# Weight pieces decoded two at a time through both banks of one PSUM tile, in an attention and MLP kernel on one Trainium2 core

## The chip, the cores and the metric

The kernel runs on one core of a Trainium2 chip. The core has TensorE (PE, matrix products), VectorE (DVE), ScalarE (ACT), GpSimd (POOL) and SyncE (SP, which only issues transfers here), each with a queue of its own that works in order; they meet through semaphores. SBUF is the memory on the core, PSUM the accumulators' memory, which is divided into banks of 512 fp32 columns. The metric is the device time of one execution in microseconds (us); lower is better.

## The reference

```python
# attention: B, H, S, D = 4, 8, 576, 64, top 32 scores of each row
scores = (q @ k.T) / sqrt(D)
kth = np.partition(scores, -32, axis=-1)[..., -32:-31]
scores = np.where(scores >= kth, scores, -1e9)
attn = softmax(scores)
x = (attn @ v)            # -> (2304, 512)
# first MLP, w_in (512, 2048), w_out (2048, 512)
h = x @ w_in
x = (h * sigmoid(h)) @ w_out
# second MLP, same sizes
h = x @ w_in
g = np.where(h > 0, h, np.exp(np.minimum(h, 0)) - 1)
out = g @ w_out
```

The inputs are float64, handed over as pairs of 32-bit integers, so that the kernel has to make floats of them itself.

## The kernel before

**Number format.** A float32 value is split into a high and a low fp16 part, and a product is three matmuls (high x high, high x low, low x high).

**Weights.** The four weight matrices come as 64 pieces (four matrices j, 16 pieces n each). A raw piece is 128 x 1024 int32, 512 KB: 512 numbers of two words per partition. Three VectorE operations decode it to 128 x 512 floats: L258 masks and shifts the high words into `y`, L262 ORs three bits of the low words into `y`, L265 takes the sign from the high words and writes the result `f`. `y` is a PSUM tile of the pool `ps_h` in slots 2 to 12, and `f` itself in the slots before and after. Then ScalarE squares the piece for a norm (L158), later scales it (L161), and GpSimd splits it into fp16 parts (L300, L164), in place in the large tile `W`, so that its row of raw words can take the next piece. Seven pieces of the last matrix are too late to find a place of their own; they come as two halves of 256 columns each (`halves`), most of which are staged in tiles of the MLP (t, gh, u, xt).

**The order of the work** is written out by hand: `slot(s)` records what the engines do in slot s, and the engines' queues keep this order. A slot has one attention tile out of 144 (18 chunks of 128 rows x 8 heads): the scores S by TensorE (L463), four rounds of MAX (L495) and MATCH_REPLACE (L499) on VectorE to find the 32nd largest, the exp on ScalarE (L510), the mask on VectorE (L523). `dv` interleaves the operations of tile s (list `a`) with those of tile s-1 (list `b`), and behind each of the eight sets `per` operations of the list `dec`, the slot's share of the decode. `d0` to `d3` say in which slot each piece is decoded: matrix 0 in slots -3 to 1, matrix 1 in slots 1 to 4, matrix 2 in 5 to 8, matrix 3 in 9 to 13.

**The MLP** begins in slot 13 (layer 0, LAG) and 25 (layer 1, LAG + LAG2). A slot has at most one step: 48 matmuls into a PSUM tile `h` of one bank (L633, 128 x 512), which ScalarE reads twice (L647 and L648 in layer 0, L652 and L653 in layer 1: first `u<-h`, then `t<-h`); GpSimd makes `t` of the two (L661), ScalarE and GpSimd make its fp16 parts `gh` (L665, L164), and 12 matmuls two slots later add it to the chunk's sum `a` (L681). Four steps make a chunk of a layer; then ScalarE copies `a` out to `o` (L694 or L725), before the next chunk may begin its sum. TensorE's order in a slot is `h`, `av` (the attention's product with V, L577), `a`, S of the next tile.

The pool `ps_h` has two buffers of one bank, so a step may write one while ScalarE still reads the other. In the decode the same two buffers hold the `y` of two neighbouring pieces, whose operations alternate (`in_turn`).

Of the kernel before, what the change touches and what calls it, by code (L numbers as in the profile page):

```python
# [10 lines left out]
F32 = mybir.dt.float32  # L11
F16 = mybir.dt.float16
BF16 = mybir.dt.bfloat16
I32 = mybir.dt.int32
# [3 lines left out]
PSUM = bass.MemoryType.PSUM  # L18
# [13 lines left out]
def kernel(  # L32
# [23 lines left out]
    NWP = KFF  # L56
# [5 lines left out]
    def pool(name, bufs, **kw):  # L62
        return ctx.enter_context(tc.tile_pool(name=name, bufs=bufs, **kw))
# [23 lines left out]
    dram = pool("dram", 1, space=bass.MemoryType.DRAM)  # L87
    p2_p = pool("p2", 6)
    ps_s = pool("ps_s", 2, space=PSUM)
    ps_h = pool("ps_h", 2, space=PSUM)  # L90
    ps_a = pool("ps_a", 1, space=PSUM)
    ps_v = pool("ps_v", 1, space=PSUM)

    W = const.tile([128, 4 * NWP + 1, 2 * DM], F16, name="W")
    Wraw = W.bitcast(F32)
    Wi = W.bitcast(I32)
    WEND = 4 * NWP + 1
# [22 lines left out]
    def xc(ch):  # L120
        kind, b, c = chunks[ch]
        return b if kind == "f" else B + b // 2
# [85 lines left out]

    stage3 = [1, 2, 3, 4, 1, 2, 3, 4, "tt", "gg", "ux", 1, "tt", "ug", (3 * NWP, WEND - 1), "gx"]

    def stage(where):
        if isinstance(where, int):
# [8 lines left out]
    weights = [w.bitcast(I32) for w in (w_in1, w_out1, w_in2, w_out2)]  # L223
    raws = {}

    def w_load(j, n, e=None):
        if j % 2 == 0:
            r0, c0 = (n % KDM) * 128, (n // KDM) * 1024
        else:
            r0, c0 = n * 128, 0  # L230
        if j < 2:
            r = 2 * NWP + 1 + 2 * n
        elif j == 2:
            r = 3 * NWP + 1 + 2 * (n % (NWP // 2))
        elif e is None:
            r = WEND - 2 * stage3[n]
        if e is None:
            t = Wi[:, r:r + 2, :].rearrange("p a x -> p (a x)")
            m = 1024
        else:  # L240
            t = stage(stage3[n][e])
            m = 512
            c0 = e * m
        nc.sync.dma_start(out=t, in_=weights[j][r0:r0 + 128, c0:c0 + m])
        raws[j, n, e] = t

    def w_dec_ops(j, n, e=None, psum=False):
        t = raws.pop((j, n, e)).rearrange("p (x two) -> p x two", two=2)
        f = Wi[:, j * NWP + n + 1, :]
        if e is not None:  # L250
            f = f[:, e * 256:(e + 1) * 256]
        low, high = t[:, :, 0], t[:, :, 1]
        y = [f]

        def first():
            if psum:
                y[0] = ps_h.tile([128, 512], F32, tag="h", name="h").bitcast(I32)[:, 0:f.shape[1]]
            nc.vector.tensor_scalar(y[0], high, 0x07FFFFFF, 3, op0=ALU.bitwise_and, op1=ALU.logical_shift_left)  # L258

        return [  # L260
            first,
            lambda: nc.vector.scalar_tensor_tensor(  # L262
                y[0], low, 29, y[0], op0=ALU.logical_shift_right, op1=ALU.bitwise_or
            ),
            lambda: nc.vector.scalar_tensor_tensor(  # L265
                f, high, -(1 << 30), y[0], op0=ALU.bitwise_and, op1=ALU.bitwise_or
            ),
        ]
# [350 lines left out]
    def emit_in(l, ch, i):  # L619
        if (l, i) == (0, 0):  # L620

            t = small.tile([128, 1], F32, tag="c1", name="c1")
            nc.gpsimd.tensor_scalar(t, ixs[:, xc(ch):xc(ch) + 1], sW[0][1], 0.5, op0=ALU.mult, op1=ALU.mult)
            c1[ch] = t
        xt = xts[l, ch]
        ps = ps_h.tile([128, 512], F32, tag="h", name="h")
        for u in range(4):
            for kk in range(KDM):
                n = 2 * l * NWP + i * 4 + kk
                f = u * 128  # L630
                wh, wl = W[:, n, f:f + 128], W[:, n, 512 + f:512 + f + 128]
                for x, (w, z) in enumerate(((wh, kk), (wh, KDM + kk), (wl, kk))):
                    nc.tensor.matmul(  # L633
                        out=ps[:, f:f + 128],
                        lhsT=w,
                        rhs=xt[:, z, :],
                        start=(kk == 0 and x == 0),
                        stop=(kk == KDM - 1 and x == 2),
                    )
        hps[l, ch, i] = ps  # L640
# [104 lines left out]
    LAG = 13  # L745
# [8 lines left out]
    loads, sumsq, tiny, early, splits, late, low, decs = (defaultdict(list) for _ in range(8))  # L754
# [18 lines left out]
    for (b, i), t in first_use.items():  # L773
        x = dict(b=b, i=i)
# [6 lines left out]
        else:  # L781
            d = 2 if b == 1 else 4
            r = first[b] - 17 - 8 * (d - 2) + 2 * d * i
# [7 lines left out]
    for g in range(NTILE // 2):  # L791
        t = 2 * g
# [3 lines left out]
    wload, wnow = defaultdict(list), defaultdict(list)  # L796

    def w_plan(j, dec, split):
        end = max(dec.values()) + 1
        for x, s in dec.items():  # L800
            decs[s].append((j, *x))
        for n in range(NWP):
            late[max(s for x, s in dec.items() if x[0] == n)].append((partial(w_norm, j, n), None))

        def total():
            m = w_sum(j)
            due.append((m, lambda m: early[end].append(lambda: w_ops(j, m))))

        late[end - 1].append((total, None))
        for (n, _), x in spread(end, split).items():  # L810
            late[x].append((partial(w_scaled, j, n), None))
            splits[x + 1].append(partial(w_split, j, n))
        return dec

    def spread(s, counts):
        return {(n, None): s + x for n, x in enumerate(x for x, c in enumerate(counts) for _ in range(c))}

    d0 = w_plan(0, spread(-3, (3, 3, 4, 4, 2)), (4, 4, 4, 4))
    d1 = w_plan(1, spread(1, (3, 5, 5, 3)), (4, 4, 4, 4))
    d2 = w_plan(2, spread(5, (4, 4, 4, 4)), (5, 5, 6))  # L820
    halves = {8: 11, 9: 11, 10: 11, 12: 12, 13: 12, 14: 13, 15: 13}
    d3 = spread(9, (4, 4, 4, 2, 2))
    d3 = w_plan(
        3, {(n, e): s for (n, _), s in d3.items() for e in ((0, 1) if n in halves else (None,))},
        (1, 1, 1, 2, 3, 2, 3, 1, 1, 1),
    )
    late[15].append((w_const, lambda: None))
    for n in range(NWP):
        x = n, None
        wload[(-5, -5, -4, -3, -3, -2, -2, -1)[n // 2]].append((0, *x))  # L830
        wload[d1[x] - 2].append((1, *x))
        wload[d1[8 + n, None] if n < 8 else d2[n - 8, None]].append((2, *x))
        if n not in halves:
            prev = {4: 0, 5: 1, 6: 2, 7: 3, 11: 4}
            wnow[d2[15 - n, None] if n < 4 else d3[prev[n], None]].append((3, *x))
    for n, x in {8: 8, 9: 8, 10: 9, 12: 11, 13: 11, 14: 12, 15: 12}.items():
        for e in range(2):
            wnow[x].append((3, n, e))
# [3 lines left out]
    def in_turn(lists):  # L842
        return [o for x in zip_longest(*lists) for o in x if o]

    def slot(s):
# [3 lines left out]
        a = tops.get(s, [])  # L849
# [2 lines left out]
            add_up(ps_s.tile([128, 2, 512], F32, tag="S", name="S"))  # L852
        summed = [f() for f in early.pop(s, [])]
        small_ops = in_turn(summed + [f() for f in tiny.pop(s, [])])
        pieces = [w_dec_ops(*x, psum=2 <= s < LAG) for x in decs[s]]
        dec = []
        for x in range(0, len(pieces), 2):
            dec += in_turn(pieces[x:x + 2])
        per = -(-len(dec) // 8)

        def dv(*qs, more=True):
# [17 lines left out]
        for x in wload[s - 1]:  # L879
            w_load(*x)  # L880
# [18 lines left out]
        t = s - 3  # L899
# [93 lines left out]
```

## Time and profile before

| what | value |
| --- | --- |
| median of 3 runs | 1192.01 us (1189.11 to 1192.39) |
| profiled execution | 1189.11 us, span of its records 1187.1 us |
| TensorE busy | 941.5 us, 79% of the span |
| VectorE busy | 998.0 us, 84% |
| ScalarE busy | 873.5 us, 74% |
| GpSimd busy | 833.3 us, 70% |
| mean granted TensorE clock | 0.981 of full speed |

The profiled execution is one of the three runs. Its span begins with the first record of the trace and ends with the last; some 2.0 us of the measured time lie outside it. All times of a row count from the span's start. A share of busy time over the whole span says little here, since the kernel has stages: loads and decode up to about 28 us, decode with attention up to about 216 us, then attention with both MLP layers, and from about 1081 us on the MLP alone.

### The profile page before, as it was taken

Reading aid. Unit: us, or ns where it says so; the run is one execution under the profiler, and the core shown is the slowest. Engines: PE = TensorE matmul, PEld = TensorE weight load, DVE = VectorE, ACT = ScalarE, POOL = GpSimd, SP = SyncE. Lnnn points to the kernel's source line nnn. Section 1 sums busy time; section 2 is a strip of 40 time slices with the busy share of each in tenths; the row PEclk is TensorE's granted clock in tenths of the full one; section 3 lists DMA queues with packets and bytes.
Section 4 is the critical chain, followed back from the end, with each engine's and each line's share of the span. In section 5 each row is a group of like instructions: output and inputs, shape, how many; then the busy total and the mean of one; then the engine's idle time right before and its main releaser. Section 6 shows DMA issues by size and latency. Waiting matters only on the chain.

```text
span 1187.1 us, 30875 instructions
## 1 busy us (share of the span) xinstructions
PE 941.5 (79%) x11574; PEld 695.1 (59%) x11574; DVE 998.0 (84%) x2559; ACT 873.5 (74%) x1699; POOL 833.3 (70%) x1070
## 2 busy tenths in 40 slices
PE   0011112757899999999999899998999999999997
PEld 0000102545667776676767676776777777777765
DVE  6999997997888899898989898998889999995000
ACT  5557655667888788888877888887767787776664
POOL 2158977699777777777777777777776776776643
PEclk9999999878999999999999999999999999999999
DMA  9967474354467655545477555545573444443100
GB/s 307 295 185 202 125 214 104 65 96 107 97 134 123 115 90 115 113 86 110 85 127 131 113 97 102 105 85 111 114 126 64 88 79 77 89 62 69 28 4 25
DMA packets 317318, 132.45 MB, mean 112 GB/s; under 512 B 293488, under 2 KB 300656, under 8 KB 317168
## 3 DMA queue, kind: packets, MB, share of 16 engines
q1 hardware_dynamic: 317168, 130.48, 51.4%
q8 instruction: 91, 1.49, 0.5%
q14 instruction: 59, 0.48, 0.1%
HBM read 52.17 MB, written 12.19 MB: 54 GB/s over the span
## 4 chain that ended last, share of the span: by engine, by line
PE 35%; POOL 21%; DVE 14%; issue 11%; DMA 10%; ACT 7%; SPq 2%; POOLq 0%; ACTq 0%
PE a L681 15%; PE h L633 14%; POOL e L555 5%; DMA et<-e 4%; POOL t L661 4%; POOL gh L164 4%; DVE m L495 3%; PE S L463 3%; PE av L577 3%; DVE r L499 2%; DVE W L265 2%; DVE h L262 2%; DVE h L258 2%; DMA vn<-in_v_dram 2%; ACT gh L665 2%
## 5 line engine op out<-in xcount | busy, mean ns | idle before, releaser
L681 PE MATMUL a<-W,gh 128*128 128x512 f16 x1728 | 403.9, 384 | 30.0 <-ACT o L725 21.0
L633 PE MATMUL h<-xt,W 128*128 128x128 f16 x6912 | 415.5, 221 | 2.0 <-DMA xt<-x 2.0
L633 PEld LDWEIGHTS <-W 128*128 128x128 f16 x6912 | 400.3, 99 | 15.7 <-issue 5.3
L495 DVE MAX8 m<-r 128x8 f32<-128x576 f32 x432 | 312.7, 749 | 1.2
L555 POOL TENSOR_TENSOR e<-e,e 128x512 f16<-128x512 f32 x144 | 167.0, 1159 | 169.9 <-ACT e L549 167.8
L681 PEld LDWEIGHTS <-gh 128*128 128x128 f16 x1728 | 161.6, 99 | 209.6 <-issue 32.9
L463 PE MATMUL S<-kt,qt 128*128 128x288 f16 (+1 forms) x640 | 102.7, 304 | 179.4 <-DVE e L523 87.8
L164 POOL TENSOR_TENSOR gh<-t,gh 128x512 f16<-128x512 f32 x144 | 166.9, 1159 | 70.3 <-ACT gh L665 67.7
L499 DVE MATCH_REPLACE8 r<-m,r 128x576 f32<-128x576 f32 x288 | 214.1, 743 | 0.0
L661 POOL TENSOR_TENSOR t<-u,t 128x512 f32<-128x512 f32 x144 | 183.0, 1271 | 29.3 <-ACT u L655 23.4
L463 PEld LDWEIGHTS <-qt 128*128 128x128 f16 (+1 forms) x640 | 56.9, 104 | 237.1 <-issue 104.4
L665 ACT ACTIVATE gh<-t 128x512 f16<-128x512 f32 x144 | 90.1, 626 | 112.3 <-POOL t L661 111.7
L510 ACT ACTIVATE e<-S,bias,c 128x576 f32<-128x576 f32 x144 | 118.1, 820 | 51.0 <-DVE bias L508 50.9
L549 ACT ACTIVATE e<-e 128x576 f16<-128x576 f32 x144 | 97.4, 677 | 61.5 <-DVE p L133 19.1
L495 DVE MAX8 m<-S 128x8 f32<-128x576 f32 x144 | 109.5, 760 | 38.6 <-PE S L463 37.1
L523 DVE SCALAR_TENSOR_TENSOR e<-S,m,e 128x576 f32<-128x576 f32 x144 | 115.5, 802 | 0.9 <-ACT e L510 0.7
L499 DVE MATCH_REPLACE8 r<-m,S 128x576 f32<-128x576 f32 x144 | 107.7, 748 | 0.0
L577 PE MATMUL av<-vt,et 128*128 128x64 f16 (+1 forms) x2240 | 94.7, 197 | 10.6 <-DMA et<-e 10.3
L577 PEld LDWEIGHTS <-et 128*128 128x128 f16 (+1 forms) x2240 | 83.5, 103 | 16.4 <-DMA et<-e 13.5
L164 POOL TENSOR_TENSOR W<-W 128x512 f16<-128x512 f32 x64 | 74.0, 1156 | 5.4
L655 ACT ACTIVATE u<-u,c 128x512 f32<-128x512 f32 x72 | 58.6, 814 | 2.4
L133 DVE TENSOR_SCALAR p<-S 128x1 int32<-128x1 int32 x54 | 8.0, 152 | 60.0 <-PE S L175 59.5
(108 smaller groups left out, 1173.2 us busy)
## 6 DMA issues: line engine op xcount, KB each, us to landing
W<-in_moe_w_in_dram SPq DMA_DIRECT2D x32, 512.0 KB, 6.4
W<-in_moe_w_out_dram SPq DMA_DIRECT2D x25, 512.0 KB, 5.3
kn<-in_k_dram SPq DMA_DIRECT2D x16, 288.0 KB, 3.2
qn<-in_q_dram SPq DMA_DIRECT2D x64, 64.0 KB, 2.6
out_dram<-o SPq DMA_DIRECT2D x16, 256.0 KB, 2.1
vd<-v SPq DMA_DIRECT2D x12, 320.0 KB, 3.3
vt<-vd SPq DMA_DIRECT2D x24, 160.0 KB, 2.7
kd<-k SPq DMA_DIRECT2D x12, 288.0 KB, 2.2
```

Of the source, the lines that this page charges most:

```text
L164: nc.gpsimd.tensor_tensor(dst, x, hi, op=ALU.subtract)
L463: nc.tensor.matmul(out=ps[n * e:n * e + n, a, 0:HALF], lhsT=qt[:, 2 * (t % 2) + p, n * e:n * e + n], rhs=kt[:, a * HALF:(a + 1) * HALF], s ...
L495: nc.vector.max(st["m8"][:, i, :], src if i == 0 else st["r"])
L499: nc.vector.match_replace(out=fold(r) if i == 0 else r, in_to_replace=st["m8"][:, i, :], in_values=src if i == 0 else r, imm_value=LOW,)
L510: nc.scalar.activation(out=fold(e), in_=src, func=AF.Exp, scale=c[:, 0:1], bias=bias)
L523: nc.vector.scalar_tensor_tensor(e, src, st["m8"][:, n - 1, 7:8], e, op0=ALU.is_ge, op1=ALU.mult, accum_out=acc)
L555: nc.gpsimd.tensor_tensor(h[:, S + LO:2 * S], e[:, 0:SF], h[:, 0:SF], op=ALU.subtract)
L577: nc.tensor.matmul(out=o, lhsT=et[:, c, n * e:n * e + n], rhs=r, start=(i == 0), stop=(i == len(seq) - 1))
L633: nc.tensor.matmul(out=ps[:, f:f + 128], lhsT=w, rhs=xt[:, z, :], start=(kk == 0 and x == 0), stop=(kk == KDM - 1 and x == 2),)
L661: nc.gpsimd.tensor_tensor(t, u, t, op=ALU.add if l else ALU.mult)
L665: nc.scalar.activation(out=gh[:, 0, :], in_=gf[l, ch, i], func=AF.Copy)
L681: nc.tensor.matmul(out=acc, lhsT=gh[:, z, u * 128:(u + 1) * 128], rhs=W[:, n, w * 512:(w + 1) * 512], start=(m == 0 and x == 0), stop=(m = ...
```

## The change

The pool `ps_h` holds one tile `hh` of two banks. Where two neighbouring full pieces (n even, and n + 1) are decoded in one slot, three operations of 1024 columns decode both, with `y` in both banks of `hh`, or in place. Their raw words have to lie one behind the other; the places of the last matrix's first eight pieces are exchanged for that (`stage3`), and pieces are moved between slots so that pairs fall into one slot (`d0`, `d1`), which moves some loads. Pieces that come as halves or alone are no longer taken in turn with a neighbour. The MLP takes the two banks of `hh` in alternation (`turn`).

```diff
-    ps_h = pool("ps_h", 2, space=PSUM)
+    ps_h = pool("ps_h", 1, space=PSUM)
...
+    hh = ps_h.tile([128, 2, 512], F32, tag="h", name="h")
+    turn = [0]
...
-    stage3 = [1, 2, 3, 4, 1, 2, 3, 4, "tt", "gg", "ux", 1, "tt", "ug", (3 * NWP, WEND - 1), "gx"]
+    stage3 = [2, 1, 4, 3, 2, 1, 4, 3, "tt", "gg", "ux", 1, "tt", "ug", (3 * NWP, WEND - 1), "gx"]
...
-    def w_dec_ops(j, n, e=None, psum=False):
-        t = raws.pop((j, n, e)).rearrange("p (x two) -> p x two", two=2)
+    def w_dec_ops(j, n, e=None, psum=False, pair=False):
+        t = raws.pop((j, n, e))
         f = Wi[:, j * NWP + n + 1, :]
+        if pair:
+
+            r = place(j, n)
+            assert place(j, n + 1) == r + 2
+            raws.pop((j, n + 1, e))
+            t = Wi[:, r:r + 4, :].rearrange("p a x -> p (a x)")
+            f = Wi[:, j * NWP + n + 1:j * NWP + n + 3, :].rearrange("p a x -> p (a x)")
+        t = t.rearrange("p (x two) -> p x two", two=2)
...
             if psum:
-                y[0] = ps_h.tile([128, 512], F32, tag="h", name="h").bitcast(I32)[:, 0:f.shape[1]]
+                y[0] = hh.rearrange("p a x -> p (a x)").bitcast(I32)[:, 0:f.shape[1]]
...
-        ps = ps_h.tile([128, 512], F32, tag="h", name="h")
+        turn[0] ^= 1
+        ps = hh[:, turn[0], :]
...
-    d0 = w_plan(0, spread(-3, (3, 3, 4, 4, 2)), (4, 4, 4, 4))
-    d1 = w_plan(1, spread(1, (3, 5, 5, 3)), (4, 4, 4, 4))
+    d0 = w_plan(0, spread(-3, (2, 4, 4, 4, 2)), (4, 4, 4, 4))
+    d1 = w_plan(1, spread(1, (2, 6, 4, 4)), (4, 4, 4, 4))
...
-        pieces = [w_dec_ops(*x, psum=2 <= s < LAG) for x in decs[s]]
-        dec = []
-        for x in range(0, len(pieces), 2):
-            dec += in_turn(pieces[x:x + 2])
+        dec, one = [], []
+        todo = list(decs[s])
+        while todo:
+            j, n, e = todo.pop(0)
+            pair = e is None and n % 2 == 0 and (j, n + 1, None) in todo
+            if pair:
+                todo.remove((j, n + 1, None))
+            o = w_dec_ops(j, n, e, psum=2 <= s < LAG, pair=pair)
+            if pair:
+                dec += o
+            else:
+                one.append(o)
+        for x in one:
+            dec += x
```

What stands in the engines' queues is seen in the built programs. In the changed kernel's file L258, L262 and L265 have become L272, L276 and L279; L495, L499, L463 and L633 have become L509, L513, L477 and L648. A wait that is named DMAHW is for a load, PE, DVE and Activation are the engines' own.

VectorE's queue before, at the start of slot 6, at the decode of two pieces (`h` is `y`, `W` holds raw words and results):

```order
L258 TENSOR_SCALAR h<-W 128x512 [waits DMAHW7_49]
L258 TENSOR_SCALAR h<-W 128x512 [waits DMAHW0_49]
L133 TENSOR_SCALAR p_970<-S 128x1 [waits PE_49]
L495 MAX m_994<-S 128x8
L262 SCALAR_TENSOR_TENSOR h<-W,h 128x512 [waits DVE_49] x2
L499 MATCH_REPLACE r<-m_906,r 128x576
L265 SCALAR_TENSOR_TENSOR W<-W,h 128x512 [waits DVE_49] x2
```

The same place after the change:

```order
L272 TENSOR_SCALAR h<-W 128x1024 [waits DMAHW7_49,DMAHW0_49]
L137 TENSOR_SCALAR p_890<-S 128x1 [waits PE_49]
L509 MAX m_911<-S 128x8
L276 SCALAR_TENSOR_TENSOR h<-W,h 128x1024 [waits DVE_49]
L513 MATCH_REPLACE r<-m_833,r 128x576
L279 SCALAR_TENSOR_TENSOR W<-W,h 128x1024 [waits DVE_49]
```

Each two operations have become one, and the first waits for both loads.

VectorE's queue before, in slot 11, where half pieces staged in `t` and `gh` are decoded:

```order
L258 TENSOR_SCALAR h<-t 128x256
L258 TENSOR_SCALAR h<-t 128x256 [waits DMAHW1_49]
L262 SCALAR_TENSOR_TENSOR h<-t,h 128x256 [waits DVE_49]
L495 MAX m_1387<-S 128x8 [waits PE_49]
L262 SCALAR_TENSOR_TENSOR h<-t,h 128x256 [waits DVE_49]
L265 SCALAR_TENSOR_TENSOR W<-t,h 128x256 [waits DVE_49] x2
L499 MATCH_REPLACE r<-m_1293,r 128x576
```

The same place after the change:

```order
L272 TENSOR_SCALAR h<-t 128x256
L276 SCALAR_TENSOR_TENSOR h<-t,h 128x256 [waits DVE_49]
L279 SCALAR_TENSOR_TENSOR W<-t,h 128x256 [waits DVE_49]
L509 MAX m_1265<-S 128x8 [waits PE_49]
L272 TENSOR_SCALAR h<-t 128x256 [waits DMAHW1_49,DVE_49]
L276 SCALAR_TENSOR_TENSOR h<-t,h 128x256 [waits DVE_49]
L279 SCALAR_TENSOR_TENSOR W<-t,h 128x256 [waits DVE_49]
```

A half piece's operations now stand one right behind the other, each with a wait for the one before it.

TensorE's queue before, at the second group of `h` matmuls, behind the scores of the slot:

```order
L463 LDWEIGHTS qt
L463 MATMUL S<-kt,qt 128x288
L633 LDWEIGHTS W
L633 MATMUL h<-xt,W 128x128
L633 LDWEIGHTS W
```

The same place after the change:

```order
L477 LDWEIGHTS qt
L477 MATMUL S<-kt,qt 128x288
L648 LDWEIGHTS W
L648 MATMUL h<-xt,W 128x128 [waits Activation_49]
L648 LDWEIGHTS W
```

The order is the same; the group's first matmul now waits for ScalarE.

## Rows read from the trace of the kernel before

**Rows 1.** Busy time by stretch: length, PE, PEld, DVE, ACT, POOL, clock, DMA, GB/s.

```profile
28.00:147.00 119.00, 13.91 (x130) 9.86 (x131) 118.43 (x264) 73.53 (x170) 74.24 (x95) 1.00 0.68 201
...
860.00:1081.00 221.00, 219.22 (x2795) 164.27 (x2793) 211.16 (x535) 170.45 (x319) 161.71 (x212) 1.00 0.47 84
```

**Rows 2.** Table of waits, whole span: us in total, times, longest.

```profile
ACT gh L665 <- POOL t L661: 111.7, 85, 3.4
...
PE a L681 <- ACT o L725: 21.0, 12, 2.8
```

**Rows 3.** VectorE's groups by line and shape: busy us, mean ns of one.

```profile
L258 DVE TENSOR_SCALAR h<-W 128x512 int32<-128x512 int32 x38 | 24.5, 683 | 1.9 <-DMA W<-in_moe_w_out_dram 1.9
...
L258 DVE TENSOR_SCALAR h<-t 128x256 int32<-128x256 int32 x4 | 1.5, 414 | 0.0
```

**Rows 4.** VectorE's timeline at three places: start, us, operation.

```profile
84.31 1.28 DVE L262 SCALAR_TENSOR_TENSOR h<-W,h 128x512 int32<-128x512 int32 x2
85.50 0.08 DVE L499 MATCH_VALUE_LOAD r<-m,r 128x8 f32 x1
...
187.03 0.68 DVE L258 TENSOR_SCALAR h<-W 128x512 int32<-128x512 int32 x1
187.75 0.69 DVE L262 SCALAR_TENSOR_TENSOR h<-W,h 128x512 int32<-128x512 int32 x1
...
190.73 0.74 DVE L258 TENSOR_SCALAR h<-t 128x256 int32<-128x256 int32 x2
191.37 0.76 DVE L495 MAX8 m<-S 128x8 f32<-128x576 f32 x1
```

**Rows 5.** VectorE's timeline at a piece that waited for its load.

```profile
149.70 0.69 DVE L258 TENSOR_SCALAR h<-W 128x512 int32<-128x512 int32 x1 [0.57 <-DMA W<-in_moe_w_out_dram]
150.30 0.76 DVE L495 MAX8 m<-S 128x8 f32<-128x576 f32 x1
```

**Rows 6.** Timelines around 205 us: GpSimd, the transfer queue, VectorE.

```profile
202.04 1.16 POOL L164 TENSOR_TENSOR W<-W 128x512 f16<-128x512 f32 x1
...
203.22 0.81 SPq L244 DMA_DIRECT2D W<-in_moe_w_out_dram  x2
...
206.04 0.29 DVE L258 TENSOR_SCALAR W<-W 128x256 int32<-128x256 int32 x1 [5.46 <-DMA W<-in_moe_w_out_dram]
...
207.03 0.76 DVE L495 MAX8 m<-S 128x8 f32<-128x576 f32 x1
```

**Rows 7.** TensorE's timeline from 541 to 558 us.

```profile
541.30 2.84 PE L633 MATMUL h<-xt,W 128*128 128x128 f16 x48
...
544.39 2.75 PE L681 MATMUL a<-W,gh 128*128 128x512 f16 x12
...
547.47 2.84 PE L633 MATMUL h<-xt,W 128*128 128x128 f16 x48
...
552.88 4.44 PE L681 MATMUL a<-W,gh 128*128 128x512 f16 x12 [2.16 <-ACT o L725]
```

**Rows 8.** ScalarE's timeline of the same stretch.

```profile
543.14 0.59 ACT L648 ACTIVATE t<-h 128x512 f32<-128x512 f32 x1
...
548.32 0.81 ACT L510 ACTIVATE e<-S,bias,c 128x576 f32<-128x576 f32 x1
...
550.12 0.59 ACT L648 ACTIVATE t<-h 128x512 f32<-128x512 f32 x1
...
552.14 0.69 ACT L725 ACTIVATE o<-a,c 128x512 f32<-128x512 f32 x1 [0.25 <-POOL c L737]
```

**Rows 9.** First and last step of the carry: TensorE's and ScalarE's timelines.

```profile
264.38 2.84 PE L633 MATMUL h<-xt,W 128*128 128x128 f16 x48
...
266.51 0.59 ACT L648 ACTIVATE t<-h 128x512 f32<-128x512 f32 x1
...
1068.25 2.84 PE L633 MATMUL h<-xt,W 128*128 128x128 f16 x48
...
1069.86 0.59 ACT L648 ACTIVATE t<-h 128x512 f32<-128x512 f32 x1
```

More of the change, by code (lines that the diff above doesn't have):

```diff
@@ L224, with place @@
     raws = {}
+    def place(j, n):
+        if j < 2:
+            return 2 * NWP + 1 + 2 * n
+        if j == 2:
+            return 3 * NWP + 1 + 2 * (n % (NWP // 2))
+        return WEND - 2 * stage3[n]
     def w_load(j, n, e=None):
@@ L230, in w_load @@
             r0, c0 = n * 128, 0
[L231 to L236, printed above, removed]
         if e is None:
+            r = place(j, n)
             t = Wi[:, r:r + 2, :].rearrange("p a x -> p (a x)")
@@ L245, in w_load @@
         raws[j, n, e] = t
-    def w_dec_ops(j, n, e=None, psum=False):
-        t = raws.pop((j, n, e)).rearrange("p (x two) -> p x two", two=2)
+    def w_dec_ops(j, n, e=None, psum=False, pair=False):
+        t = raws.pop((j, n, e))
         f = Wi[:, j * NWP + n + 1, :]
+        if pair:
+            r = place(j, n)
+            assert place(j, n + 1) == r + 2
[3 more added lines that the diff above has]
+        t = t.rearrange("p (x two) -> p x two", two=2)
         if e is not None:
@@ L833 @@
         if n not in halves:
-            prev = {4: 0, 5: 1, 6: 2, 7: 3, 11: 4}
-            wnow[d2[15 - n, None] if n < 4 else d3[prev[n], None]].append((3, *x))
+            prev = {4: 0, 5: 1, 6: 2, 7: 3, 11: 5}
+            wnow[d2[16 - stage3[n], None] if n < 4 else d3[prev[n], None]].append((3, *x))
     for n, x in {8: 8, 9: 8, 10: 9, 12: 11, 13: 11, 14: 12, 15: 12}.items():
```

## Prediction

> **What bounds the kernel now.** I read the busy time by stretches first, because the change touches two stages that have nothing in common. While the weights are decoded, from 28 to 147 us, VectorE is busy 118.43 of 119 us and TensorE 13.91 [rows 1]: whatever VectorE saves or loses there moves everything behind it. From 860 to 1081 us TensorE is busy 219.22 of 221 us and VectorE 211.16 [rows 1]: there TensorE sets the pace, with VectorE close behind. Then the table of waits. TensorE's group `a` waited for ScalarE's copy `o` 12 times, 21.0 us in all, at most 2.8 us; ScalarE's `gh` waited for GpSimd's `t` 85 times, 111.7 us in all [rows 2]. The second row says that in the MLP stage ScalarE mostly waits for GpSimd, not for TensorE; that matters below. The prices come from timelines, since the duration of a VectorE row overlaps the next one and is not what the queue pays.
>
> **The decode, step by step.** The built programs hold 213 decode instructions before (171 of 512 columns, 42 of 256) and 129 after (84 of 1024, 3 of 512, 42 of 256): 84 fewer. 16 of these stand before slot 0, where the loads set the pace, so 68 count. The columns are the same, so what an instruction costs beside its columns is the whole gain. Two OR operations of 512 columns that don't depend on each other take 85.50 - 84.31 = 1.19 us from start to start, 0.595 each; two of 256 columns take 191.37 - 190.73 = 0.64, 0.32 each [rows 4]. The difference, 0.275 us for 256 columns, makes 0.55 us for 512 and leaves 0.045, say 0.05 us, per instruction. Gain: 68 x 0.05 = 3.4 us. The lower bound is 0. The upper bound is what the durations would give: 683 ns at 512 columns and 414 at 256 [rows 3] leave 414 - 269 = 145 ns per instruction, 68 x 0.145 = 9.9 us. I take the start-to-start price, because a queue that is 99% busy pays from start to start.
>
> Against that stands the order. Before, the operations of two pieces alternate, so an operation seldom follows its own input at once. A lone piece shows the price: its three operations start at 187.03 and 187.75 [rows 4], 0.72 us apart instead of 0.595, so 0.12 us per such neighbour. Counted in the built programs, slots 0 to 10 have 4 more of them after the change (19 for 15), slot 11 has 11 more (14 for 3), slot 12 six more, slot 13 three more; the half pieces no longer alternate. Slot 12's six cost nothing: VectorE then idles 5.46 us before 206.04 for a load whose issue, at 203.22, stands behind GpSimd's split of 202.04 [rows 6]. Without that cover they would cost 0.7 us. So 18 x 0.12 = +2.2 us. [...]
>
> A paired operation also waits for the later of its two loads. At 149.70 the second piece's first operation had waited 0.57 us for its load, after the first piece's was already done, and the next operation came at 150.30 [rows 5]. Paired, 1024 columns begin at 149.70 and end some 2 x 0.55 + 0.05 = 1.15 us later, at 150.85: +0.55 us. One place like it, early in slot 0, gets the same: +1.1 us. In slot 13 the reverse happens: the halves are no longer paired, so the MAX at 207.03 no longer waits for the load of the second half; behind the operation of 206.04 [rows 6] stands one more of 256 columns, so that it begins 2 x 0.32 us later, at about 206.7: -0.3 us. Decode in all: -3.4 + 2.2 + 1.1 - 0.3 = -0.4 us.
>
> **The handover of h.** This part is not in the words of the change. One tile `hh` holds both banks now. In the built program 141 of 144 groups of `h` matmuls wait for ScalarE's last read of the group just before (the `t<-h` activation); before, the second buffer let a group start while the one before was still read. So the MLP loses its second buffer, although the banks alternate. The price is seen around 541 us. TensorE's own pace is 547.47 - 541.30 = 6.17 us per slot [rows 7]. The step ahead of 541.30 is read by ScalarE until 543.14 + 0.59 = 543.73 [rows 8], so the `h` of 541.30 would start at 543.73, 2.43 us late. The read of that step ends at 550.71 [rows 8], so the next `h` starts there instead of 547.47, 3.24 us late. Its `a` is then due 550.71 + (544.39 - 541.30) = 553.80, and finds `o` copied: that copy began at 552.14 and took 0.69 [rows 8]. Before, the same `a` stood 2.16 us waiting for it and then ran 4.44 us instead of 2.75, at a lower clock [rows 7]. So this `a` is over at 553.80 + 2.75 = 556.55, where it was at 557.3: the new waits have only replaced the wait for `o`.
>
> This needs ScalarE's own times to stay. They do as long as TensorE's delay does not come back to ScalarE: its `gh` waits for GpSimd [rows 2], its read at 550.12 is of the group that would start at 543.73 and be over 2.84 us later, at 546.6; and the exp of the scores that stood ready at 541.30 began only at 548.32 [rows 8], 7.0 us later, of which VectorE needs three operations of 0.76 [rows 4], 2.3 us, ahead of it: a delay of the scores by 2.4 us finds 4.7 us of cover. Carried step by step from the `h` of 264.38 against the read of 266.51 to the `h` of 1068.25 against the read of 1069.86 [rows 9], `h` would start before the read of the step ahead is over in 93 of some 140 steps; carried, that leaves 62 waits, about 54 us in all, most under 1 us, seven over 2 us. Nearly all end in slots where TensorE idles before anyway. Only in the stretch in which TensorE is busy throughout [rows 1] is nothing there to take them: by the carry 1.5 us stay from 900 us on, and 0.5 us come in the last steps, where three groups stand back to back. So +2 us.
>
> **Sum.** -0.4 + 2 = +1.6 us on the profiled execution's 1189.1, whose span is 1187.1 with 2.0 us around it: 1190.7. That execution is the fastest of three, 2.9 us under their median of 1192.01; on the median the forecast is 1193.5. Under 0.3% (3.6 us) is about what a measurement of this kernel can't tell from no change.
>
> **The rivals.** *Slower, the handover is not absorbed.* One mechanism: TensorE's wait for `t<-h` delays the scores, these delay VectorE's MAX, mask and bias, and ScalarE, which works through them in order, reads `h` later in turn; then each wait is paid again. It decides where the delay exceeds the cover, which is 4.7 us at the step above and less where ScalarE is less far behind. For it: VectorE is 95% busy in the last stretch [rows 1], so it can't catch up. Against it: most waits of the carry are under 1 us. In part, with the seven waits over 2 us each followed by a group at the lower clock (4.44 - 2.75 = 1.7 us, [rows 7]): 7 x 1.7 = 12 us, 1205. In full, 54 us: 1246. Chances 0.23 and 0.08.
>
> *Faster, the fixed price is the larger one.* If an instruction costs 0.145 us beside its columns, as durations have it [rows 3], the decode gives -9.9 + 2.2 + 1.1 - 0.3 = -6.9, and with +2 for `h` the time is 4.9 us under before, 1187. Against it is the start-to-start price [rows 4]. [...] Chance 0.17.
>
> *No effect at all of the handover* (the wait is there but always met): -0.4 us, 1191.6, within my own case.
>
> **How the numbers follow.** No change that can be measured: 0.52, the likeliest, at 1193.5 with its own range of 1188 to 1197. Faster 0.17, slower 0.31 (the two slower cases). The range of 8 in 10 takes in the faster rival at 1187 and the partial slower one at 1205, each with a little room, and leaves out the full price.
>
> **What the changed profile would show.** The 1024-column OR should take about 683 + 512 x 1.05 = 1221 ns; starts 1.12 us apart mean that the fixed price is as I took it. Half pieces of slot 11 should stand one behind the other. In the waits a new row, TensorE's `h` for ScalarE's `t`, should appear with about 60 waits and some 50 us, while `a` for `o` falls from 21.0 us to a few; from 300 to 1081 us the stretch should be no more than 2 us longer. If that new row is there and the stretch is 10 us longer, I was wrong about the cover; if the first matmuls of the MLP start 5 us earlier, I was wrong about the price of an instruction.

## The result, and the profile after

The changed kernel takes 1200.82 us (median of 4 runs, 1200.28 to 1204.28), beside 1191.47 us for the kernel before (4 runs). The ratio is 1.0084, 95% interval 1.0068 to 1.0101: 9 to 10 us slower. That lies inside the stated range, but it is not the likeliest case, "no change that can be measured" at 1193.5 us; it is nearest to the partial slower rival at 1205. The profiled execution took 1200.83 us with a span of 1199.0 us, 11.9 us above the span before.

Where do the 11.9 us arise? Each slot has one MAX that reads new scores (L509, before L495), so its start is a clock of the program. The table gives its start minus that of the same slot's MAX in the kernel before, in us, for the changed kernel and for five kernels of the experiments; the last row is the span.

```
slot               0     11     12     14     36     72    116    143    span
before         28.17 177.71 191.37 216.12 369.02 609.76 906.55 1074.62 1187.1
changed         2.72   1.39   2.86   2.38   4.62   6.70   6.80    9.85   11.9
two buffers     1.93   0.42   1.88   1.56   3.01   3.14   3.47    3.46    3.7
one tile        0.40   5.53   6.60   6.53   9.10   9.43   9.86   14.84   15.1
plain start     0.56  -1.07   0.40   0.07   4.31   9.19  10.93   14.16   14.2
halves in turn  1.87   0.16   0.16  -0.18   1.72   1.91   2.21    2.08    2.2
all three      -0.73  -2.40  -2.41  -2.50   0.51   0.74   2.45    2.73    2.2
```

In the changed kernel 2.7 us are there before slot 0, the decode gives back 0.3 up to slot 14, and the MLP loses 9.5 from there to the end. Of the forecast -0.4 for the decode, +0.55 belonged to slot 0's start; the other terms add up to -0.95, so the decode gave back less than forecast. Most of the start was not forecast, and the MLP is far from the forecast +2.

First VectorE's prices. Groups by line and shape, then the timeline at two of the places of [rows 4]:

```profile
L272 DVE TENSOR_SCALAR h<-W 128x1024 int32<-128x1024 int32 x19 | 23.1, 1216 | 3.7 <-DMA W<-in_moe_w_out_dram 3.0 <-DMA W<-in_moe_w_in_dram 0.7
L276 DVE SCALAR_TENSOR_TENSOR h<-W,h 128x1024 int32<-128x1024 int32 x19 | 23.0, 1212 | 0.1
```

```profile
84.57 1.21 DVE L276 SCALAR_TENSOR_TENSOR h<-W,h 128x1024 int32<-128x1024 int32 x1
85.69 0.08 DVE L513 MATCH_VALUE_LOAD r<-m,r 128x8 f32 x1
...
193.44 0.41 DVE L272 TENSOR_SCALAR h<-t 128x256 int32<-128x256 int32 x1
193.89 0.43 DVE L276 SCALAR_TENSOR_TENSOR h<-t,h 128x256 int32<-128x256 int32 x1
194.23 0.76 DVE L509 MAX8 m<-S 128x8 f32<-128x576 f32 x1
```

The OR of 1024 columns lasts 1212 ns (1221 were forecast) and takes 85.69 - 84.57 = 1.12 us from start to start, where two of 512 took 1.19 [rows 4]: the fixed price of an instruction is small, as taken. The halves now stand one right behind the other: 0.45 us from 193.44 to 193.89, where 0.32 was the price of a half in turn [rows 4].

Then the waits, which answer to [rows 2], from the table of waits (us in total, times, longest):

```profile
ACT gh L680 <- POOL t L676: 97.2, 83, 3.3
...
ACT e L524 <- DVE bias L522: 70.5, 59, 7.8
...
DVE m L509 <- PE S L477: 55.8, 61, 5.7
PE h L648 <- ACT t L663: 27.4, 25, 6.1
...
PE h L648 <- ACT t L668: 21.7, 22, 2.3
```

The new wait is there: TensorE's `h` waits for ScalarE's `t<-h` 47 times, 49.1 us in all. Its wait for the copy `o`, 21.0 us before [rows 2], no longer appears in the table. The carry of the prediction had 62 waits and 54 us, so it had their amount nearly right; what it had wrong is what they cost. Two other rows have grown, and the same table of the kernel before shows from where:

```profile
ACT e L510 <- DVE bias L508: 50.9, 38, 9.2
DVE m L495 <- PE S L463: 37.1, 43, 4.5
```

VectorE's MAX waits 19 us more for TensorE's scores, and ScalarE's exp 20 us more for the bias that VectorE makes of them. Both are steps of the way by which a delay of TensorE comes back to ScalarE.

The busy time by stretch, as in [rows 1] (length, PE, PEld, DVE, ACT, POOL, clock):

```profile
28.00:147.00 119.00, 13.01 (x121) 9.15 (x122) 115.02 (x206) 73.98 (x171) 73.58 (x93) 1.00 0.69 204
867.00:1090.00 223.00, 220.11 (x2794) 164.15 (x2792) 210.07 (x531) 171.74 (x319) 162.09 (x213) 1.00 0.44 84
```

TensorE is still busy 99% of the late stretch, which holds as many matmuls as that of [rows 1] but is 2 us longer. A share of busy time doesn't show such a loss.

### The profile page after: what moved, and what is told of

It reads as the page before. It is cut to its first block, busy times and chain, and to the rows that moved or that the text cites. A ratio compares the mean times of both kernels' runs of the same rounds, so it can differ in the third digit from the quotient of the medians.

```text
span 1199.0 us, 30759 instructions
## 1 busy us (share of the span) xinstructions
PE 940.0 (78%) x11574; PEld 696.7 (58%) x11574; DVE 994.5 (83%) x2475; ACT 875.4 (73%) x1699; POOL 834.4 (70%) x1070
## 3 DMA queue, kind: packets, MB, share of 16 engines
q8 instruction: 90, 1.47, 0.5%
## 4 chain that ended last, share of the span: by engine, by line
PE 28%; POOL 23%; DVE 16%; issue 13%; DMA 10%; ACT 8%; SPq 1%; POOLq 0%; ACTq 0%; DVEq 0%
PE h L648 13%; PE a L696 11%; DMA et<-e 6%; POOL e L569 6%; POOL t L676 5%; POOL gh L168 4%; DVE m L509 4%; DVE r L513 3%; DVE h L276 2%; DVE h L272 2%; PE S L477 2%; PE av L591 2%; DVE W L279 2%; DMA W<-in_moe_w_in_dram 2%; ACT gh L680 2%
## 5 line engine op out<-in xcount | busy, mean ns | idle before, releaser
L648 PE MATMUL h<-xt,W 128*128 128x128 f16 x6912 | 417.5, 221 | 52.1 <-ACT t L663 27.4
L648 PEld LDWEIGHTS <-W 128*128 128x128 f16 x6912 | 403.9, 99 | 70.4 <-issue 63.1
L696 PE MATMUL a<-W,gh 128*128 128x512 f16 x1728 | 396.6, 379 | 0.7 <-POOL gh L168 0.6
L509 DVE MAX8 m<-r 128x8 f32<-128x576 f32 x432 | 312.5, 748 | 1.2
L477 PE MATMUL S<-kt,qt 128*128 128x288 f16 (+1 forms) x640 | 103.1, 304 | 181.0 <-DVE e L537 92.1
L513 DVE MATCH_REPLACE8 r<-m,r 128x576 f32<-128x576 f32 x288 | 213.7, 742 | 0.0
L477 PEld LDWEIGHTS <-qt 128*128 128x128 f16 (+1 forms) x640 | 56.9, 104 | 237.5 <-issue 104.4
L509 DVE MAX8 m<-S 128x8 f32<-128x576 f32 x144 | 109.5, 760 | 56.6 <-PE S L477 55.8
L513 DVE MATCH_REPLACE8 r<-m,S 128x576 f32<-128x576 f32 x144 | 107.6, 747 | 0.0
```

The lines of the kernel that those rows point to most:

```text
L477: nc.tensor.matmul(out=ps[n * e:n * e + n, a, 0:HALF], lhsT=qt[:, 2 * (t % 2) + p, n * e:n * e + n], rhs=kt[:, a * HALF:(a + 1) * HALF], s ...
L509: nc.vector.max(st["m8"][:, i, :], src if i == 0 else st["r"])
L513: nc.vector.match_replace(out=fold(r) if i == 0 else r, in_to_replace=st["m8"][:, i, :], in_values=src if i == 0 else r, imm_value=LOW,)
L648: nc.tensor.matmul(out=ps[:, f:f + 128], lhsT=w, rhs=xt[:, z, :], start=(kk == 0 and x == 0), stop=(kk == KDM - 1 and x == 2),)
L696: nc.tensor.matmul(out=acc, lhsT=gh[:, z, u * 128:(u + 1) * 128], rhs=W[:, n, w * 512:(w + 1) * 512], start=(m == 0 and x == 0), stop=(m = ...
```

## The experiments

Theory H after the result: the lost second buffer of `h` costs the MLP's 9.5 us. Rival D: the shifted start and the decode did it, by moving transfers and ScalarE's side work against the MLP.

**Two buffers for the MLP again.** The changed kernel, with the tile of two banks given up before slot 13 and two separate one-bank buffers from then on.

```diff
...
-        turn[0] ^= 1
-        ps = hh[:, turn[0], :]
+        if not ps_h:
+            early_psum.close()
+            ps_h.append(pool("ps_h", 2, space=PSUM))
+        ps = ps_h[0].tile([128, 512], F32, tag="h", name="h")
```

> The changed kernel, but the MLP gets two separate one-bank buffers for h again (the decode keeps its tile of two banks, which is given up before slot 13). Theory H: the lost second buffer costs the MLP stage what the two traces show there, from 2.4 us at the scores of slot 14 to 11.9 us at the end, 9.5 us. Then this run is some 9 us under the changed kernel, at 1191 to 1194 us, and the lag against the kernel before stays at about 2.4 us from slot 14 to the end. Rival D: the lag in the MLP comes from the shifted start and from the decode, which put the transfers and ScalarE's side work at other places against the MLP. Then it stays near 1200.

1193.83 us, ratio 1.0016 (1.0004 to 1.0028); against the changed kernel's 1.0084 that is 0.7%, 8 us (7.0 between the medians). From slot 14 to slot 143 it loses 1.9 us (table), the changed kernel 7.5. The old wait is back and the new one gone:

```profile
PE a L698 <- ACT o L742: 20.4, 12, 2.8
```

H holds: the handover is the larger part of the loss. Rival D is out. A loss of 1.9 to 5.2 us from slot 14 to slot 143 is seen in all four kernels without the handover (the two-buffer kernels of the table, and the plan alone below): the profiled execution of before is one of its faster ones, and single executions scatter. It arises up to slot 116. From slot 116 to slot 143 these four kernels lose -0.1 to +0.3 us, and the three with one tile 3.05 (changed), 5.0 (one tile) and 3.2 (plain start).

**One tile alone.** The kernel before, with the tile of two banks, whose halves alternate, for `h` and for `y`; operations and their order are untouched.

```diff
+    def h_half():
+        turn[0] ^= 1
+        return hh[:, turn[0], :]
...
-                y[0] = ps_h.tile([128, 512], F32, tag="h", name="h").bitcast(I32)[:, 0:f.shape[1]]
+                y[0] = h_half().bitcast(I32)[:, 0:f.shape[1]]
...
-        ps = ps_h.tile([128, 512], F32, tag="h", name="h")
+        ps = h_half()
```

> The kernel before, with one tile of two banks for h instead of two buffers; the decode's operations and their order are untouched. Theory H: 7 to 10 us slower than before, 1198 to 1201 us. The carry of the prediction: 2 us slower, 1193.5. Rival D: as before, 1191.5.

1206.78 us, ratio 1.0129 (1.0105 to 1.0153), above the 1198 to 1201 us that H gave. The MLP loses 8.6 us from slot 14 to the end, as H has it. The decode loses 6.1 us besides, from slot 0 to slot 14, which I had not expected: with one tile the operations of the second piece wait for those of the first. In the built program 51 operations of slots 0 to 10 wait for the one right before them, where the kernel before has 15. The lag grows by 5.1 us there, 0.14 us for each of the 36: the 0.12 us of the prediction, measured in another way. Its timeline shows two ORs with such a wait, which answer to the 1.19 us of [rows 4]:

```profile
98.03 1.40 DVE L269 SCALAR_TENSOR_TENSOR h<-W,h 128x512 int32<-128x512 int32 x2
99.35 0.08 DVE L506 MATCH_VALUE_LOAD r<-m,r 128x8 f32 x1
```

1.32 us for two, 0.13 more. So a single tile has two prices, and the pairs of the change are also what spares it the second one.

**The plan alone, and a plain start.** Two runs ask what makes the start late: the kernel before with only the new plan of pieces (`d0`, `d1`), and the changed kernel with single, alternating operations up to slot 0.

```diff
-            pair = e is None and n % 2 == 0 and (j, n + 1, None) in todo
+            pair = s > 0 and e is None and n % 2 == 0 and (j, n + 1, None) in todo
...
-        for x in one:
-            dec += x
+        for x in range(0, len(one), 2):
+            dec += in_turn(one[x:x + 2]) if s <= 0 else sum(one[x:x + 2], [])
```

> The kernel before, with only the plan of the change: matrix 0 decoded 2, 4, 4, 4, 2 pieces a slot from slot -3 and matrix 1 2, 6, 4, 4, unpaired. Theory P: the start's 2.7 us come from this plan, which puts fewer pieces into slot -3; then the first MAX of scores comes 2 to 3 us later than before and the time is 1193 to 1194.5. Rival: they come from the paired operations; then the first MAX comes as before (28.2 us) and the time is 1191.5.

> The changed kernel, but with single, alternating operations of 512 columns up to slot 0 and pairs from slot 1 on. If pairing causes the start's 2.7 us: the first MAX of scores comes at about 28.2 us instead of 30.9, and the time is 1198 to 1199.5. If the plan causes them: 30.9 and 1200.8 as in the changed kernel.

The plan alone: 1193.23 us, ratio 0.9996 (0.9980 to 1.0012), its slot 0 is 0.84 us earlier than before. The plain start: slot 0 is at +0.56 us instead of +2.72. So pairing makes the start late, not the plan; the plan by itself was expected to move slot 0 by 0 or by 2 to 3 us, and neither came. In time the plain start shows nothing, 1201.65 us, ratio 1.0074 (1.0058 to 1.0091): the interval allows the 2 us as well as none, and its MLP lost more in the profiled execution (table). The next two kernels differ in the plain start alone.

The way of the delay is read from the timeline of all engines (POOL is GpSimd, SPq the transfer queue). The changed kernel, up to slot 0:

```profile
8.48 0.69 DVE L272 TENSOR_SCALAR W<-W 128x1024 int32<-128x1024 int32 x1 [3.62 <-DMA W<-in_moe_w_in_dram]
...
12.06 2.83 POOL L168 TENSOR_TENSOR k<-kn,k 128x512 f16<-128x512 f32 x2 [11.62 <-ACT k L366]
...
12.66 2.06 DVE L276 SCALAR_TENSOR_TENSOR W<-W 128x1024 int32<-128x1024 int32 x1
...
14.85 1.66 POOL L168 TENSOR_TENSOR q<-qn,q 128x256 f16<-128x256 f32 x1
...
16.54 1.29 SPq L461 DMA_TRANSPOSE qt<-q  x1
...
23.35 1.87 SPq L250 DMA_DIRECT2D W<-in_moe_w_in_dram  x4
...
30.00 0.96 DVE L272 TENSOR_SCALAR W<-W 128x1024 int32<-128x1024 int32 x1 [3.98 <-DMA W<-in_moe_w_in_dram]
```

and the same steps before:

```profile
11.86 1.86 POOL L164 TENSOR_TENSOR k<-kn,k 128x512 f16<-128x512 f32 x2 [11.42 <-ACT k L352]
13.69 1.12 POOL L164 TENSOR_TENSOR q<-qn,q 128x256 f16<-128x256 f32 x1
...
14.84 1.30 SPq L447 DMA_TRANSPOSE qt<-q  x1
...
21.82 1.86 SPq L244 DMA_DIRECT2D W<-in_moe_w_in_dram  x4
...
27.64 0.60 DVE L258 TENSOR_SCALAR W<-W 128x512 int32<-128x512 int32 x1 [0.80 <-DMA W<-in_moe_w_in_dram]
```

The paired operations in SBUF and GpSimd's splits of k and q run at the same time and both get longer: the splits take 2.83 and 1.66 us instead of 1.86 and 1.12 (2.09 and 0.85 in the kernel with the plain start), and the OR beside them 2.06 instead of 1.23. The transposes wait for the splits, and the next four weight loads stand behind the transposes in the transfer queue, so they are issued 1.5 us later. Slot 0's first pair waits for the later of its two loads until 30.00. Before, the second piece of slot 0 waited for the same load until 27.64: it comes 2.36 us later, 1.5 of them by the issue. From there to the slot's MAX it takes 0.89 us in the changed kernel and 0.53 before, so waiting for both loads at once costs only some 0.4 us here.

**The halves in turn again, and all three mended.** Two kernels with two buffers from slot 11 on and the halves in turn; the second with the plain start too.

```diff
...
-        for x in one:
-            dec += x
+        for x in range(0, len(one), 2):
+            dec += in_turn(one[x:x + 2])
...
```

> The changed kernel with two buffers of one bank for h from slot 11 on (pairs before that in one tile of two banks), and with the half pieces of slots 11 to 13 in turn again. If a neighbour that follows its own input costs 0.12 us, slot 11 and slot 13 get 1.3 to 1.7 us shorter than with the halves one behind the other: the lag against the kernel before grows by about 0 instead of 1.5 us at slot 12, and the time is 1192 to 1192.5, against 1193.8 of the run with two buffers alone. If such a neighbour costs nothing: 1193.8.

> As the run beside it (two buffers from slot 11 on, halves in turn), and single, alternating operations up to slot 0, pairs from slot 1 on. If the pairs up to slot 0 cost 2.2 us through their wait for the later of two loads, and pairs from slot 1 on gain 1.6 us: 1190 to 1191.5, that is 1 to 3 us under the kernel before. If pairs gain nothing by themselves: 1192.8 as before.

Halves in turn: 1191.91 us, ratio 1.0001 (0.9988 to 1.0013). The lag from slot 11 to 14 is -0.34 us instead of +1.14, so the order of the halves was worth 1.5 us. All three: 1190.09 us, ratio 0.9981 (0.9968 to 0.9994), 2.3 us under the kernel before, with slot 0 at -0.73 us instead of +1.87. In time the two medians lie 1.8 us apart, and the means of their twelve runs 1.7 (0.2 to 3.3): the start counts, by an amount that is not well known. This is the fastest kernel of the study. From slot 0 to slot 11 its pairs gain 1.7 us; they gain the same in the kernel with the plain start.

**TensorE's order, to move the reads against the groups.** Both kernels with `h` behind `av` and `a` in each slot.

```diff
+        if 0 <= t < NTILE:
+            emit_av(t)
+        if p2:
+            emit_out(*p2)
         if cur:
             emit_in(*cur)
...
```

> The changed kernel, but TensorE does a slot's av and a groups ahead of its h group (order av, a, h, S instead of h, av, a, S). Theory L: the single buffer costs because ScalarE ends its read of h some 5.5 us after the group has ended, which is more than the 3.3 us that lie between the end of one group and the start of the next; with h 3.2 us later in the slot and ScalarE's own work where it was, the read ends 2.3 us after the group, in time. Then TensorE's waits for t<-h fall from 49 us to under 15, and the difference to the kernel before with the same order is 1 to 4 us instead of 9. Rival: ScalarE's reads are tied to TensorE's own progress and move along with h; then the waits stay near 49 us and the difference near 9 us. The a groups come earlier too, so both kernels may wait more for the copy o.

> The kernel before with the same order av, a, h, S: the control of the run beside it. Its a groups stand 2.84 us earlier in the slot, so waits for the copy o may grow from 21 to some 40 us, of which a part was cover before: 1191 to 1200 us. Both theories expect the same of this run; they differ in how far the changed kernel with this order stands above it.

1364.82 us (ratio 1.1446, 1.1422 to 1.1469) and 1367.90 us (1.1484, 1.1458 to 1.1511). The order made both kernels wait elsewhere: ScalarE's `u` now waits for TensorE's `h`, 194 us in the changed kernel with this order. The waits for `t<-h` are all but gone (1.3 us) and the two kernels no longer differ to the handover's disadvantage, as theory L has it. But another loop bounds both now: from 700 to 1000 us TensorE is busy 262 of 300 us in each, where it was 291 before. So the pair is no test of L.

**ScalarE's reads ahead of its `gh`.** Both kernels, and the fastest one, with the two exchanged.

```diff
-        if p1:
-            emit_ghi(*p1)
-            emit_glo(*p1)
         if cur:
             emit_act(*cur)
+        if p1:
+            emit_ghi(*p1)
+            emit_glo(*p1)
```

> The changed kernel, with ScalarE's reads of h (u and t of step n) ahead of its gh of step n-1, instead of behind it. In the traces the loop gh, u, t, u, u on ScalarE, then t on GpSimd, then gh again takes 6.63 us in a layer-1 slot, against TensorE's 6.17; without gh in it, it takes some 6.1. Theory F: the single buffer costs because ScalarE falls behind by 0.46 us in each such slot and so ends its read of h after TensorE could start the next group; TensorE then passes the delay on through the scores to ScalarE's exp in the slots in which ScalarE has caught up. With the shorter loop, TensorE's waits for t<-h fall from 49 us to under 20, and the run stands at most 4 us above the control beside it. Rival: the waits come from the bunches of ScalarE's side work (k, v, q and x parts), not from this loop; then the waits stay over 35 us and the difference stays at 7 to 9 us.

> The kernel before with the same exchange: the control. ScalarE no longer waits for GpSimd in the loop, so it may be a little faster than before, 1185 to 1192. A later gh could make TensorE's a group wait: then up to 1195.

> The fastest kernel so far (two buffers for h from slot 11 on, halves in turn, pairs from slot 1 on) with the same exchange: 2 us under the control beside it, as that kernel without the exchange stood 2.3 us under the kernel before.

1281.75 us (ratio 1.0746, 1.0720 to 1.0772), 1277.40 (1.0724, 1.0704 to 1.0743) and 1275.48 (1.0710, 1.0690 to 1.0730). The expected gain was wrong in sign: with a later `gh`, GpSimd's part of it comes later, and GpSimd's `e` and `t` stand behind that in its queue, so ScalarE waits for `t` in both kernels (200 us in the changed one, 192 in its control). The fastest kernel with the exchange stands 1.9 us under its control, near the expected 2, but the intervals overlap. The waits of the changed kernel with this order:

```profile
ACT u L667 <- POOL t L676: 106.9, 63, 3.4
ACT u L662 <- POOL t L676: 93.1, 50, 3.6
...
PE h L648 <- ACT t L663: 48.9, 35, 3.8
PE h L648 <- ACT t L668: 41.8, 48, 1.8
```

and two of its control's:

```profile
PE a L681 <- POOL gh L164: 31.5, 50, 2.2
PE a L681 <- ACT o L725: 31.4, 16, 3.8
```

TensorE waits 90.7 us for `t<-h`, nearly twice as long as in the changed kernel, and yet stands only 0.2% above its control (the intervals overlap). Theory F's number for the waits (under 20 us) is refuted, and so is its rival's 7 to 9 us of difference. In the control TensorE's group `a` waits for GpSimd's and ScalarE's results instead, 81 us in all with two smaller rows; in the changed kernel with this order these waits are 8 us. Here the new waits have replaced old ones almost in full, which is what the prediction expected of the change itself. What the pair does show: where the loop of ScalarE and GpSimd bounds the kernel, the same handover costs next to nothing, so its price is not the sum of its waits.

**y in SBUF.** The fastest kernel, with `y` in place in SBUF in all slots.

```diff
-            o = w_dec_ops(j, n, e, psum=2 <= s < LAG, pair=pair)
+            o = w_dec_ops(j, n, e, pair=pair)
```

> The fastest kernel so far (two buffers for h from slot 11 on, halves in turn, pairs from slot 1 on), with y in SBUF instead of PSUM in all slots. The first operation of a pair takes 678 ns with its result in SBUF and 1215 ns with it in PSUM, in that kernel's trace: 19 pairs by 0.54 us, 10.2 us, and some 1 us for the halves. If that passes through: 1179 to 1181. Rival: next to GpSimd's splits the operations in SBUF are held up: in the changed kernel one OR in SBUF at 12.7 us took 2.06 us instead of 1.23, and GpSimd's two k splits 2.83 us where two others took 1.42. GpSimd is busy 74 of the 119 us of the decode, so 5 to 10 us can go that way: 1185 to 1191.

1216.97 us, ratio 1.0207 (1.0188 to 1.0225): worse than the rival's worst case. Groups by shape of this kernel, VectorE's over the whole span and GpSimd's conversion, the first half of a split, from 28 to 216 us:

```profile
L281 DVE TENSOR_SCALAR W<-W 128x1024 int32<-128x1024 int32 x21 | 19.9, 948 | 12.9 <-DMA W<-in_moe_w_in_dram 10.1 <-DMA W<-in_moe_w_out_dram 2.8
L285 DVE SCALAR_TENSOR_TENSOR W<-W 128x1024 int32<-128x1024 int32 x21 | 31.6, 1503 | 0.1
...
L323 POOL TENSOR_SCALAR W<-W 128x512 f16<-128x512 f32 x43 | 40.8, 950 | 3.2 <-ACT W L171 0.3
```

and GpSimd's of the same stretch in the kernel with `y` in PSUM:

```profile
L323 POOL TENSOR_SCALAR W<-W 128x512 f16<-128x512 f32 x48 | 29.7, 618 | 3.6 <-ACT W L171 0.3
```

The first operation of a pair is shorter in SBUF (948 ns for 1215), but the OR is longer (1503 for 1212), GpSimd's conversion goes from 618 to 950 ns, and VectorE's pairs wait 12.9 us for loads. The timeline of the kernel with `y` in SBUF shows that the two engines do this to each other:

```profile
124.64 1.15 POOL L174 TENSOR_TENSOR W<-W 128x512 f16<-128x512 f32 x1
124.74 2.13 DVE L285 SCALAR_TENSOR_TENSOR W<-W 128x1024 int32<-128x1024 int32 x1
...
132.49 2.24 POOL L174 TENSOR_TENSOR W<-W 128x512 f16<-128x512 f32 x1
132.52 1.20 DVE L285 SCALAR_TENSOR_TENSOR W<-W 128x1024 int32<-128x1024 int32 x1
...
142.90 0.62 POOL L323 TENSOR_SCALAR W<-W 128x512 f16<-128x512 f32 x1
```

Once the OR beside a split takes 2.13 us, once the split beside an OR takes 2.24 instead of 1.15. The three ORs with no GpSimd operation beside them take 1206 to 1226 ns, as in PSUM, and at 142.90, while VectorE idles, GpSimd's conversion is back at 0.62 us. The longest of VectorE's waits for loads, 10.12 us before 148.44, is for a load that was issued at 142.39, right behind a transpose of `et`, which waited for GpSimd's `e` that ended at 141.0 behind a row of splits.

## Why the prediction was right or wrong

**The decode's prices were right, two waits were missed.** The price of 0.05 us for an instruction: between the MAXs of slots 0 and 11 the kernel with the plain start has 63 instructions fewer and gains 1.63 us, while VectorE's idle time there grows from 2.9 to 4.9 us. So its work shrinks by 3.6 us, and with two more neighbours (0.3 us) that is 3.9 / 63 = 0.06 us for an instruction. The faster rival, 0.145 us, is out. The 2.0 us of new idle time are 0.66 for the later load of slot 7's pair, 0.67 more than before for slot 8's, the place of [rows 5] (+0.55 forecast), 0.60 for scores in slot 2, which the kernel with the plan alone has too, and small gaps. So some 1.3 us of the gain became waiting that the prediction had not listed. The neighbours were worth 0.12 us by the prediction and 0.14 in the kernel with one tile, whose trace has 1.32 us for two ORs with such waits, where the kernel before has 1.19 for two without [rows 4]. Slot 11 lost 1.47 us (1.3 forecast).

**The start was wrong.** The step that failed is "16 of these stand before slot 0, where the loads set the pace, so 68 count". It took the time of the loads as given, and left +0.55 us for slot 0's pair, of which 0.4 were seen. The loads do set the pace there, but their issue hangs on GpSimd's splits, which the paired operations made longer (4.5 us together instead of 3.0), and the load that slot 0 waits for came 2.4 us later. The start is 2.2 to 2.7 us late in place of 0.55; the kernels with the plain start have it back.

**The handover was seen, and its price was mis-sized.** That the built program makes each group wait for the read just before it, that this replaces the wait for `o`, and the amount of waiting were right. The step that failed is "This needs ScalarE's own times to stay. They do as long as TensorE's delay does not come back to ScalarE", with 4.7 us of cover from one slot. That slot is one in which ScalarE is behind. In nearly every cycle of eight slots there are others in which it has caught up and its exp waits for the bias: of the 38 waits of the kernel before, 26 stand in slots 25 to 143, with 22 of the 50.9 us. There the cover is nothing. In the changed kernel these slots have 46 such waits, 41 us. An example is slot 39 (VectorE, then ScalarE):

```profile
394.82 0.77 DVE L509 MAX8 m<-S 128x8 f32<-128x576 f32 x1 [1.13 <-PE S L477]
...
397.25 0.83 ACT L524 ACTIVATE e<-S,bias,c 128x576 f32<-128x576 f32 x1 [2.04 <-DVE bias L522]
...
399.07 0.59 ACT L663 ACTIVATE t<-h 128x512 f32<-128x512 f32 x1
```

and the same exp and read before:

```profile
392.63 0.83 ACT L510 ACTIVATE e<-S,bias,c 128x576 f32<-128x576 f32 x1 [1.07 <-DVE bias L508]
...
394.46 0.59 ACT L648 ACTIVATE t<-h 128x512 f32<-128x512 f32 x1
```

The exp waits 1 us longer. From the read of `h` one step earlier (392.04, before 388.58) to this one the lag of ScalarE's reads goes from 3.46 to 4.61 us, up to that of VectorE's MAX of the scores, 4.62 (394.82, before 390.20): until then the delay was TensorE's and VectorE's, from there on it is ScalarE's too, and the next cycle starts from it and adds its own. So what the carry took as one loss (1.5 us from 900 us on) comes again in each cycle: from slot 116 to 143 the lag of the changed kernel grows by 3.05 us, with steps of up to 0.7 us in the slots 119, 125 to 127, 133 to 135 and 141 to 143, of which some 0.6 us each are given back at slots 128 and 136. The other two kernels with one tile lose 5.0 and 3.2 us there, most of it in the same slots; with two buffers nothing is lost.

To the end the changed kernel loses 2.05 us more, where 0.5 was forecast. This is mostly something else (changed kernel, then before):

```profile
1168.68 4.47 PE L648 MATMUL h<-xt,W 128*128 128x128 f16 x48 [2.07 <-DMA xt<-x]
1174.41 2.84 PE L648 MATMUL h<-xt,W 128*128 128x128 f16 x48 [1.26 <-ACT t L668]
```

```profile
1158.94 8.21 PE L633 MATMUL h<-xt,W 128*128 128x128 f16 x144 [2.00 <-DMA xt<-x]
```

After an idle time of 2.07 us for a load, one group of `h` took 4.47 us instead of 2.84: the granted clock was 0.50 of full speed from 1169.0 to 1172.4, for 3.4 us. After a like wait of 2.00 us before the change it was 1.00 from 1158.94 to 1167.20. That is 1.6 of the 2.05 us; the other two kernels with one tile have no such group there and lose 0.0 and 0.2 us after slot 143. Why the clock fell in this execution is open.

In all the handover costs 7 to 8 us (two buffers against one), where 2 were forecast. The way through the scores is the one that the slower rival named. It is read from the traces and not isolated: the two pairs of runs that were meant for it got other bounds. The rival's price, seven waits each followed by a group at a lower clock, is not what happened: after 300 us the changed kernel has the one such group of 1168.68, the kernel before three (at 337.45, 552.88 and 714.14, of 4.29 to 4.44 us, at a granted clock of 0.50 for a part of each; [rows 7] has the second), and the mean granted clock is 0.986 after and 0.981 before. That the time came out nearest to this rival's 1205 is luck: a late start and a loss that returns in each cycle brought it there.

How the handover's loss spreads over the MLP is less certain than its sum. By the table 4.4 us arise in the changed kernel from slot 14 to 116, but 1.9 to 5.0 arise there in the kernels without the handover too, and 10.9 in the one with the plain start. Only the stretch from slot 116 on tells one tile from two buffers in a single execution.

## What to carry to other kernels

Alternating the halves of one tile by hand is no double buffer where the program keeps its waits per tile (here TensorE waited 49.1 us for `t<-h`, and the kernel took 7 to 8 us longer than with two buffers): look in the built program for what the next writer waits for. When a new wait is laid over old ones, don't take its cover from the slot in which the reader is furthest behind; look through a whole cycle for the slots in which it has caught up and waits for the delayed engine itself, since there the delay passed to all engines here and stayed (3.05 us from slot 116 to 143). An operation that takes two loads waits for the later one, so a part of what it saves can turn into waiting (here some 0.4 us in slot 0 of the changed kernel, and 0.66 and 0.67 us in slots 7 and 8 with the plain start). And where loads set the pace, ask what their issue waits for: an operation that makes another engine's work longer can make the loads late (here the splits of k and q took 4.5 us instead of 3.0, and the loads behind them were issued 1.5 us later).

## What was not expected of the hardware

VectorE's decode with all operands in SBUF and GpSimd's splits held each other up where both ran: with `y` in SBUF, VectorE's OR of 1024 columns took 1503 ns in the mean and up to 2196 (1212 with `y` in PSUM), and GpSimd's conversion of 512 columns 950 ns (618). Alone, the OR in SBUF took 1206 to 1226 ns. With its result in PSUM the first operation of the decode was longer by itself (1215 ns, where the three in SBUF with no GpSimd operation beside them took 675 to 682), and yet the kernel is 27 us faster, 1190.09 us for 1216.97. No run here tells whether the operand that `y` is read from or the one it is written to matters.
